# Routed attention and a gated FFN on one core: one-hot columns turned apart from the split keys and queries, values loaded from Pool's queue, a second FFN output bank

## The chip, the cores and the metric

The kernel runs on one core of a Trainium2 chip. The core has a matrix engine (PE, with its weight loads listed apart as PEld), three engines for elementwise work (DVE, ACT, POOL), a queue engine without arithmetic (SP), 16 DMA engines that all queues share, an on-chip memory of 128 partitions (SBUF), and an accumulator memory (PSUM) of eight banks of 128 partitions x 512 fp32, which PE alone writes with matmuls. Each engine runs its own instructions in order and waits for others by semaphores. The metric is the device time of one execution in microseconds.

## What is computed

Attention in which a query sees only the keys of its own cluster, followed by a gated feed-forward network. B = 4 batches, H = 8 heads, S = 768 positions, D = 64, 16 centroids for each head; 3072 tokens, model width 512, inner width 1536; all fp32.

```python
q_assign = np.argmax(np.einsum('bhsd,hcd->bhsc', q_n, c_n), axis=-1)
k_assign = np.argmax(np.einsum('bhsd,hcd->bhsc', k_n, c_n), axis=-1)
mask = q_assign[:, :, :, None] == k_assign[:, :, None, :]
scores = np.where(mask, scale * np.matmul(q, k.transpose(0, 1, 3, 2)), -1e9)
attn = np.exp(scores - scores.max(-1, keepdims=True))
x = tokens_of(np.matmul(attn / (attn.sum(-1, keepdims=True) + 1e-9), v))
gate = 1.0 / (1.0 + np.exp(-(x @ w_gate)))
return gate * (x @ w_val) @ w_out
```

The last line stands for `(gate * val) @ w_out`; `tokens_of` moves the heads side by side.

## The kernel before

**Clusters as extra rows.** For each head the kernel builds a tile T: 128 rows for each position, in chunks of 128 positions. Rows 0 to 63 are the key or query in fp16. Rows 64 to 127 first hold what fp16 lost of it (hi and lo, made by `split`: DVE casts, POOL subtracts). From all 128 rows PE computes the 16 logits of each position (`logits2`, L226, in the first batch, 36 matmuls for each pair of heads; `logits`, L240, later, 12 for each head). DVE picks the largest (`pick`, L252) and writes a one-hot of 16 columns for a key, and -1920 times its complement for a query, over the first 16 lo columns of the same position-major tile `hl`. Scores then use rows 0 to 79 of T, so the mask comes out of the same matmul. As `hl` is position-major and T is row-major, `turn` (L219) sends it through a DMA transpose from SP's queue. It does so twice for each tile: once for the logits, once more with the one-hots in it:

```python
SP.dma_start_transpose(out=T[key], in_=hl.rearrange("p c x -> p (c x)"))
```

**Steps.** `run_steps` goes over score steps. A step is one score matmul (128 keys x 384 queries, L399), an exponential on ACT (L404), and, two steps later, three matmuls with the values (L416). The first batch runs as 48 steps on the first halves of the queries (kind "A") and 48 on the second ("B"); each further batch has 96 steps, 12 for each head. In this count the second batch begins at step 96. After the last step of a head POOL normalises (L200), after each second head a DMA transpose from SP makes the FFN's input xA, xB or xT.

**What is hung between the steps.** `at(i, f)` puts work behind step i in program order: loads, splits, turns, logits, picks, sums of the values, weight loads. The order of each engine is the program order. In the first batch a pair of heads has one T of 18 chunks for A (12 of keys, 6 of queries) and one of 6 for B. From the second batch on, `head_prep` (L535) starts 30 steps ahead of use: split, four steps on the first turn, at 12 the logits, at 13 pick and second turn, both of 12 chunks. A pair's keys, queries and values are loaded 80 steps ahead from SP's queue. The weights come from POOL's queue (fp32 in memory, fp16 in SBUF): behind steps 8, 20, 25, 31 a third of gate and value weights each comes in four parts, behind 37 and 43 the output weights.

**FFN.** From step 60 on, matmuls of the FFN of finished tokens are spread between the steps (`ffn_run`, with a cost for each piece): gates (L281, tanh on ACT L287), values (L296, product on DVE L301), outputs in three parts of four matmuls (L313, eviction on ACT L322 or DVE L320, store from SP). What is left of the last batch runs after its attention.

**PSUM.** `ring` (L66) is a ring of five banks, used in turn by scores, gates, values, logits and value sums; a bank can be written again when its reader is done. `avp` has two banks for the products with the values, `op` (L68) one for the FFN output.

**Start.** PE warms up on 14 matmuls of zeros (`dummies`), the centroids are normalised (`centroid_prep`, L133), then come split, turns and logits of pairs 0 and 1.

## Time and profile before

| | |
|---|---|
| median of 2 runs | 420.66 us (419.72 and 421.6) |
| the profiled execution | 421.55 us, of which the span is 419.8 us |
| PE busy | 338.0 us, 81% of the span |
| ACT busy | 230.1 us, 55% |
| DVE busy | 172.8 us, 41% |
| POOL busy | 109.1 us, 26% |
| DMA, SP's queue | 51.17 MB, packets' time 57.2% of 16 engines' span |
| DMA, POOL's queue | 4.72 MB, 8.6% |

The span runs from the first instruction to the last; what lies around it is 1.75 us. Busy shares are means over stages that differ, so they are read by stage. A wait is idle time of an engine, put down to what ended it. A DMA share above 1 means that packets of several queues were under way on an engine at once. The granted clock of PE is given as a share of 2.4 GHz; 0.5 is 1.2 GHz.

### The profile page before, as it was taken

The page shows a single profiled execution, that of the slowest core. Times are in us where ns is not written, and L with a number is a line of the kernel's source. Part 1 is how long each engine was busy: PE and PEld are TensorE (multiplying, and loading weights), DVE is VectorE, ACT ScalarE, POOL GpSimd, SP SyncE. Part 2 cuts the span into 40 slices and gives each one's busy share as a digit, 9 for nine tenths or more (in the row PEclk, how much of TensorE's full clock was granted, in tenths as well). Part 3 has the DMA queues.
Part 4 walks back from the last instruction along what each step waited for, and adds up shares of the span by engine and source line. Part 5 has one row for each costly group of instructions (what it writes and reads, how often), then busy time and mean ns, then how long its engine had stood idle before and what let it go on. Part 6 is the DMA issues. An engine that isn't in the chain of part 4 may idle for free.

```text
span 419.8 us, 8423 instructions
## 1 busy us (share of the span) xinstructions
PE 338.0 (81%) x3129; PEld 205.4 (49%) x3129; DVE 172.8 (41%) x441; ACT 230.1 (55%) x524; POOL 109.1 (26%) x174
## 2 busy tenths in 40 slices
PE   5166801619999688768999989999999899899995
PEld 1135501406665355444456656664666566465552
DVE  1332301302573446463455646572656443133230
ACT  2034600527875667675577767775887678143230
POOL 1653520300433142351324242323233200000000
PEclk9565665556999989896999999999999999999999
DMA  8999999991677958797877688587465831200201
GB/s 298 267 164 131 171 182 164 123 243 39 161 163 172 202 108 196 144 183 146 175 168 193 153 161 229 107 207 138 96 123 96 147 84 20 69 27 0 78 0 75
DMA packets 135769, 58.78 MB, mean 140 GB/s; under 512 B 114736, under 2 KB 132656, under 8 KB 135728
## 3 DMA queue, kind: packets, MB, share of 16 engines
q1 hardware_dynamic: 128304, 51.17, 57.2%
q0 software_dynamic: 5792, 4.72, 8.6%
q10 hardware_dynamic: 1632, 2.36, 1.6%
q8 instruction: 24, 0.39, 0.4%
q14 instruction: 17, 0.14, 0.1%
HBM read 28.34 MB, written 6.29 MB: 83 GB/s over the span
## 4 chain that ended last, share of the span: by engine, by line
PE 49%; DMA 12%; DVE 2%; issue 1%; ACT 1%; SPq 0%; POOL 0%; DVEq 0%; ACTq 0%; POOLq 0%
PE o L313 13%; DMA T<-hl 12%; PE g L281 11%; PE v L296 11%; PE sc L399 8%; PE av L416 4%; PE lg L243 2%; ACT ob L322 1%; ACT es L404 1%; DVE ob L320 1%; DVE hl L265 0%; SPq L224 0%; DVE hT L301 0%; POOL hl L215 0%; PE vs_ps L167 0%
## 5 line engine op out<-in xcount | busy, mean ns | idle before, releaser
L404 ACT ACTIVATE es<-sc 128x384 f16<-128x384 f32 x384 | 174.6, 493 | 105.2 <-PE sc L399 88.0
L399 PE MATMUL sc<-T 80*128 80x384 f16 x384 | 128.4, 359 | 1.8 <-DMA T<-hl 1.8
L416 PEld LDWEIGHTS <-es 128*128 128x128 f16 x1152 | 86.5, 104 | 52.9 <-ACT es L404 7.9
L416 PE MATMUL av<-va,es 128*128 128x65 f16 x1152 | 104.9, 203 | 2.0 <-ACT es L404 1.3
L301 DVE SCALAR_TENSOR_TENSOR hT<-th,v 128x384 f16<-128x384 f32 x96 | 53.0, 553 | 91.2 <-PE av L416 49.5
L313 PE MATMUL o<-wo,hT 128*128 128x512 f16 x288 | 71.0, 378 | 5.5 <-DVE ob L320 2.9
L200 POOL TENSOR_TENSOR xp<-t,rec 128x384 f16<-128x384 f32 (+1 forms) x40 | 27.9, 697 | 160.8 <-DVE rec L197 136.3
L287 ACT ACTIVATE th<-g 128x384 f32<-128x384 f32 x96 | 47.3, 493 | 26.8 <-DVE hT L301 16.2
L281 PE MATMUL g<-xTb,wg 128*128 128x384 f16 x288 | 58.6, 325 | 0.1
L296 PE MATMUL v<-xTb,wv 128*128 128x384 f16 x288 | 58.6, 325 | 0.0
L281 PEld LDWEIGHTS <-wg 128*128 128x128 f16 x384 | 38.1, 99 | 22.6 <-issue 2.4
L296 PEld LDWEIGHTS <-wv 128*128 128x128 f16 x384 | 38.1, 99 | 22.2 <-issue 2.4
L215 POOL TENSOR_TENSOR hl<-kraw,hl 128x384 f16<-128x384 f32 x32 | 29.4, 924 | 73.9 <-issue 44.6
L313 PEld LDWEIGHTS <-hT 128*128 128x128 f16 x288 | 27.8, 97 | 33.2 <-issue 8.0
L399 PEld LDWEIGHTS <-T 80*128 80x128 f16 x384 | 39.2, 103 | 3.5 <-DMA T<-hl 2.7
L233 PE MATMUL lg<-cm,T 128*128 128x16 f16 x192 | 6.5, 175 | 42.1 <-DMA T<-hl 42.1
L215 POOL TENSOR_TENSOR hl<-qraw,hl 128x384 f16<-128x384 f32 (+1 forms) x40 | 30.4, 767 | 17.0 <-DVE hl L212 16.9
L195 DVE TENSOR_TENSOR t<-av,sv 128x390 f32<-128x390 f32 (+1 forms) x40 | 19.2, 480 | 25.3 <-PE av L416 25.3
L233 PEld LDWEIGHTS <-T 128*128 128x128 f16 x192 | 5.9, 105 | 43.3 <-DMA T<-hl 43.3
L243 PE MATMUL lg<-cm,T 128*128 128x32 f16 x288 | 11.1, 177 | 17.4 <-DMA T<-hl 17.2
L322 ACT ACTIVATE ob<-o 128x512 f32<-128x512 f32 x16 | 9.6, 597 | 26.2 <-PE o L313 26.1
L212 DVE CAST hl<-qraw 128x384 f16<-128x384 f32 (+1 forms) x40 | 13.9, 364 | 20.0 <-DMA T<-hl 20.0
(52 smaller groups left out, 206.5 us busy)
## 6 DMA issues: line engine op xcount, KB each, us to landing
kraw<-in_k_dram SPq DMA_DIRECT2D x16, 384.0 KB, 4.3
out_dram<-ob SPq DMA_DIRECT2D x24, 256.0 KB, 2.5
vraw<-in_v_dram SPq DMA_DIRECT2D x14, 384.0 KB, 5.2
qraw<-in_q_dram SPq DMA_DIRECT2D x12, 384.0 KB, 4.2
qraw<-in_q_dram ACTq DMA_DIRECT2D x4, 384.0 KB, 6.9
wg<-in_moe_w_gate_dram POOLq DMA_DIRECT2D x4, 384.0 KB, 9.6
wv<-in_moe_w_val_dram POOLq DMA_DIRECT2D x4, 384.0 KB, 11.9
wo<-in_moe_w_out_dram POOLq DMA_DIRECT2D x2, 768.0 KB, 12.7
```

What stands on the lines that cost most here:

```text
L195: DVE.tensor_tensor(t[:, 0:nq, :], av, sv, ALU.add)
L200: (eng or POOL).tensor_tensor(x, t[:, 0:nq, 0:64], bcast(rec[:, 0:nq], 64), ALU.mult)
L215: POOL.tensor_tensor(hl[:, o : o + m, 64:128], r, hl[:, o : o + m, 0:64], ALU.subtract)
L243: PE.matmul(out=lg[:, bass.ts(c, 32)], lhsT=T[key][:, c, :], rhs=cm[:, h].rearrange("p s n -> p (s n)"), start=True, stop=True,)
L281: PE.matmul(out=g[:, 0:n], lhsT=wg[fc // WQ][:, dc, fc % WQ, :], rhs=xT[:, dc, t0 : t0 + n], start=(dc == 0), stop=(dc == NDC - 1),)
L287: ACT.activation(th[:, 0:n], g[:, 0:n], AF.Tanh, scale=0.5)
L296: PE.matmul(out=w[:, 0:n], lhsT=wv[fc // WQ][:, dc, fc % WQ, :], rhs=xT[:, dc, t0 : t0 + n], start=(dc == 0), stop=(dc == NDC - 1),)
L301: DVE.scalar_tensor_tensor(hT[:, fc, 0:n], st[0][:, 0:n], 1.0, w[:, 0:n], ALU.add, ALU.mult)
L313: PE.matmul(out=o, lhsT=hT[:, fc, bass.ts(t, 128)], rhs=wo[fc // 6][:, fc % 6, :], start=(fc == 0), stop=(fc == NFC - 1),)
L399: PE.matmul(out=sc.rearrange("p (c t) -> p c t", t=128), lhsT=s["k"], rhs=s["q"], start=True, stop=True,)
L404: ACT.activation(es, sc, AF.Exp, scale=SCALE)
L416: PE.matmul(out=av[:, s["c0"] + i, :], lhsT=s["es"][:, bass.ts(i, 128)], rhs=VA[b, p][:, e, s["j"], :], start=(first and i == 0), stop=(la ...
```

## The change

**One-hots apart.** The one-hots no longer go into `hl`. `pick` writes them into tiles of their own, `oh` (three tiles of 128 x 6 chunks x 128, zeroed once), in which each head has 32 columns for keys and 32 for queries, two heads to a tile. Turned, they lie in rows 0 to 15, 32 to 47, 64 to 79 and 96 to 111 of `ohT`, and only those 16 rows are put into rows 64 to 79 of T, by `hop`: a DMA from SP of 16 partitions x 768 or 384 fp16 values. T is thus turned once for the logits and keeps rows 0 to 63.

- First pair: PE transposes 64 columns of `oh` at a time into PSUM, DVE and ACT copy 16 rows of it into T (`first_place`). No DMA.
- Pairs 1 to 3 of A, all of B: PE transposes, DVE copies PSUM to `ohT`, four or two hops (`a_place`, `b_place`).
- From the second batch on: one DMA transpose of 6 chunks for each pair of heads, then four hops (`pair_prep`). Splits begin 58 steps ahead of use (48 for the second head), keys and queries apart, the turn 9 steps after the split, the logits 20, the one-hots' turn 26 steps ahead of use, the hops 16 and 15.

**First batch.** T of A is now made for each head (9 chunks) instead of for each pair (18). The first head's lo part is subtracted on DVE. The order of the start is new: keys and queries of pair 0 are loaded first, those of pairs 2 and 3 behind the first turns, values from POOL's queue; 8 dummies, then 14 behind the centroids, and 2 twice. The weights are behind steps 14, 26, 30, 34, and 40 and 46. The splits of B are behind steps 20, 27, 34, 41, their turns 3 later, logits 14, hops 17. Later loads are 76 steps ahead of use.

**Pools.** `hl` 3 to 4, `T` 7 to 10 tiles (of 12 chunks at most, before 18), `ohT` two; the PSUM ring 5 to 4 banks, `op` 1 to 2.

SP's queue at the start of the program (k, q, v raw are the loaded inputs; T<-hl a turn; T<-ohT a hop). Before:

```order
L96 DMA cen<-in_centroids_dram 128x64
L93 DMA kraw<-in_k_dram 128x2x384 x3
L93 DMA vraw<-in_v_dram 128x2x384
L93 DMA kraw<-in_k_dram 128x2x384
L93 DMA vraw<-in_v_dram 128x2x384
L224 DMA_TRANSPOSE T<-hl 128x18x128 x7
L424 DMA_TRANSPOSE xA<-xp 128x3x128
```

After:

```order
L95 DMA kraw<-in_k_dram 128x2x384
L100 DMA cen<-in_centroids_dram 128x64
L95 DMA kraw<-in_k_dram 128x2x384
L222 DMA_TRANSPOSE T<-hl 128x9x128 x2
L95 DMA kraw<-in_k_dram 128x2x384
L95 DMA qraw<-in_q_dram 128x2x384
L222 DMA_TRANSPOSE T<-hl 128x9x128 x2
L95 DMA kraw<-in_k_dram 128x2x384
L95 DMA qraw<-in_q_dram 128x2x384
L287 DMA T<-ohT 16x768
L287 DMA T<-ohT 16x384
```

Two more hops and the four turns of heads 4 to 7 follow. The value loads are gone from here, four loads moved behind turns, and the turns of heads 4 to 7 stand behind the hops of pair 1.

POOL from the first values to the first weights (va are values cast to fp16, xp normalised outputs, hl lo parts). Before:

```order
L154 MEMSET va 128x12
L155 CAST va<-vraw 128x12x64
L215 TENSOR_TENSOR hl<-kraw,hl 128x6x64 x2
L215 TENSOR_TENSOR hl<-qraw,hl 128x3x64 x2
L200 TENSOR_TENSOR xp<-t,rec 128x3x64
L113 DMA wg_149<-in_moe_w_gate_dram 128x4x384
L113 DMA wv_150<-in_moe_w_val_dram 128x4x384
```

After:

```order
L95 DMA vraw<-in_v_dram 128x2x384 x2
L156 MEMSET va 128x12
L157 CAST va<-vraw 128x12x64
L202 TENSOR_TENSOR xp<-t,rec 128x3x64
L215 TENSOR_TENSOR hl<-kraw,hl 128x6x64
L215 TENSOR_TENSOR hl<-qraw,hl 128x3x64
L215 TENSOR_TENSOR hl<-kraw,hl 128x6x64
L215 TENSOR_TENSOR hl<-qraw,hl 128x3x64
L202 TENSOR_TENSOR xp<-t,rec 128x3x64
L114 DMA wg_137<-in_moe_w_gate_dram 128x4x384
L114 DMA wv_138<-in_moe_w_val_dram 128x4x384
```

The first weights now stand behind the output of the second head instead of the first, and the last two value loads stand ahead of them.

SP's queue in the second batch, one pair of heads. Before:

```order
L224 DMA_TRANSPOSE T<-hl 128x12x128 x2
L424 DMA_TRANSPOSE xTb<-xp 128x6x128
L224 DMA_TRANSPOSE T<-hl 128x12x128 x2
L93 DMA kraw<-in_k_dram 128x2x384
L93 DMA qraw<-in_q_dram 128x2x384
L93 DMA vraw<-in_v_dram 128x2x384
```

After:

```order
L95 DMA kraw<-in_k_dram 128x2x384
L95 DMA qraw<-in_q_dram 128x2x384
L95 DMA vraw<-in_v_dram 128x2x384
L645 DMA_TRANSPOSE ohT<-oh_153 128x6x128
L222 DMA_TRANSPOSE T<-hl 128x12x128
L444 DMA_TRANSPOSE xTb<-xp 128x6x128
L287 DMA T<-ohT 16x768 x4
L222 DMA_TRANSPOSE T<-hl 128x12x128
```

Four turns of 12 chunks became two, one of 6 chunks and four hops.

The diff, cut:

```diff
-    tp = pool("T", 7)
+    tp = pool("T", 10)
+    ohp = pool("oh", 2)
-    ring = pool("ring", 5, space=bass.MemoryType.PSUM)
+    ring = pool("ring", 4, space=bass.MemoryType.PSUM)
-    op = pool("op", 1, space=bass.MemoryType.PSUM)
+    op = pool("op", 2, space=bass.MemoryType.PSUM)
...
-        hl = HL[key]
-        for parts, alu in ((kparts, ALU.is_equal), (qparts, ALU.is_lt)):
-            for a, z in parts:
-                DVE.tensor_tensor(
-                    hl[:, a:z, 64:80], lg[:, a:z], bcast(mx[:, a:z], NCL), alu
-                )
-        for a, z in qparts:
-            DVE.tensor_scalar(hl[:, a:z, 64:80], hl[:, a:z, 64:80], MASK, None, ALU.mult)
+        for a, z, nh, key, o in parts:
+            DVE.tensor_tensor(
+                o,
+                lg[:, a:z].rearrange("p (h c) n -> p h c n", h=nh),
+                bcast(mx[:, a:z].rearrange("p (h c) -> p h c", h=nh), NCL),
+                ALU.is_equal if key else ALU.is_lt,
+            )
+            if not key:
+                DVE.tensor_scalar(o, o, MASK, None, ALU.mult)
...
+    def oh_turn_pe(oh, nc_):
+        ps = bank(NCH * 128, HP, name="oh_ps")
+        for c in range(nc_):
+            PE.transpose(ps[:, bass.ts(c, 128)], oh[:, c, :], identh)
+        return ps
+
+    def hop(src, slot, t, c0, n):
+        SP.dma_start(
+            out=t[64:80, c0 : c0 + n, :], in_=src[32 * slot : 32 * slot + 16, 0:n, :]
+        )
...
+    def first_place(e, oh):
+        ps = bank(NCH * 128, HP, name="oh_ps")
+        for c in range(NCH):
+            PE.transpose(ps[64 * e : 64 * e + 64, bass.ts(c, 128)], oh[:, c, 64 * e : 64 * e + 64], identh)
+        t = T["A", e]
+        pv = ps.rearrange("p (c t) -> p c t", t=128)
+        DVE.tensor_copy(t[64:80, 0:6, :], pv[64 * e : 64 * e + 16, :, :])
+        ACT.copy(t[64:80, 6:9, :], pv[64 * e + 32 : 64 * e + 48, 0:3, :])
...
+    def a_place(p):
+        ps = oh_turn_pe(st0["oh", p], NCH)
+        ot = ohp.tile([128, NCH, 128], HP, tag="ohT", name="ohT")
+        DVE.tensor_copy(ot.rearrange("p c t -> p (c t)"), ps)
+        for e in range(2):
+            hop(ot, 2 * e, T["A", 2 * p + e], 0, 6)
+            hop(ot, 2 * e + 1, T["A", 2 * p + e], 6, 3)
...
+    at(0, lambda: a_logits(1))
+    at(1, lambda: a_pick(1))
+    at(3, lambda: a_place(1))
+    at(4, lambda: (a_turn(4), a_turn(5)))
...
+    at(9, lambda: (a_turn(6), a_turn(7)))
+    at(12, lambda: a_logits(2))
...
+    at(14, lambda: load_w(0))
...
+    at(26, lambda: load_w(1))
     for p in range(NP):
-        s = 22 + 6 * p
+        s = 20 + 7 * p
         at(s, lambda p=p: b_split(p))
-        at(s + 2, lambda p=p: turn(("B", p), tbp, True))
-        at(s + 12, lambda p=p: b_logits(p))
-        at(s + 13, lambda p=p: b_pick(p))
-    at(25, lambda: load_w(2))
-    at(31, lambda: load_w(3))
-    at(37, lambda: load_wo(0))
-    at(43, lambda: load_wo(1))
...
+        at(s + 3, lambda p=p: b_turn(p))
+        at(s + 14, lambda p=p: b_logits(p))
+        at(s + 15, lambda p=p: b_pick(p))
+        at(s + 17, lambda p=p: b_place(p))
+    at(30, lambda: load_w(2))
+    at(34, lambda: load_w(3))
+    at(40, lambda: load_wo(0))
+    at(46, lambda: load_wo(1))
...
+        for e in range(2):
+            s = use - 58 + 10 * e
+            at(s, lambda e=e: sp(e, 0))
+            at(s + 4, lambda e=e: sp(e, 1))
+            at(s + 9, lambda e=e: turn((b, 2 * p + e), st["hl", e], tp))
+            at(s + 20, lambda e=e: lgt(e))
+            at(s + 21, lambda e=e: pk(e))
+        at(use - 26, ot)
+        at(use - 16, lambda: hops(0))
+        at(use - 15, lambda: hops(1))
```

## Rows read from the trace of the kernel before

**Rows 1.** Sums by stage: stretch; busy PE, PEld, DVE, ACT, POOL (count); PEclk, DMA, GB/s

```profile
0.00:26.90 26.90, 10.85 (x99) 5.14 (x99) 8.61 (x30) 2.97 (x4) 10.59 (x22) 0.68 0.96 249
26.90:99.80 72.90, 35.52 (x379) 24.34 (x380) 14.45 (x53) 28.53 (x61) 21.90 (x38) 0.56 1.02 163
99.80:127.90 28.10, 28.09 (x277) 17.82 (x276) 15.62 (x42) 21.40 (x50) 9.21 (x15) 0.98 0.56 138
127.90:203.00 75.10, 59.67 (x614) 36.68 (x610) 37.28 (x92) 49.28 (x118) 24.18 (x36) 0.89 0.78 168
203.00:357.40 154.40, 148.21 (x1461) 91.92 (x1462) 80.28 (x196) 111.68 (x260) 42.35 (x63) 1.00 0.66 137
357.40:419.80 62.40, 55.65 (x312) 29.51 (x308) 16.52 (x30) 16.23 (x32) 0.82 (x1) 0.99 0.12 42
```

**Rows 2.** The same sums for the score matmuls (L399) alone: PE, PEld

```profile
26.90:99.80 72.90, 27.19 (x61) 7.47 (x61) 0.56 1.02 163
```

**Rows 3.** Waits of PE, 26.9 to 99.8 us: total, times, longest

```profile
PE lg L233 <- DMA T<-hl: 32.0, 4, 18.7
```

**Rows 4.** Timeline: start, length, engine, line, instruction, count, idle before and releaser

```profile
18.70 1.13 PE L233 MATMUL lg<-cm,T 128*128 128x16 f16 x36 [9.21 <-DMA T<-hl]
...
22.41 2.72 PE L469 MATMUL wm<-warm 128*128 128x512 f16 x6
...
26.93 0.34 PE L399 MATMUL sc<-T 80*128 80x384 f16 x1 [1.79 <-DMA T<-hl]
...
35.17 0.94 POOL L113 DMA_DIRECT2D wg<-in_moe_w_gate_dram  x1
```

**Rows 5.** DMA from 13 to 34 us: rate in 40 slices; issues, us to landing

```profile
GB/s 377 375 372 190 181 205 222 215 214 179 209 218 217 217 171 1 0 5 201 209 150 1 9 168 290 286 289 290 288 93 102 215 214 216 220 158 0 0 103 216
...
T<-hl SPq DMA_TRANSPOSE x6, 4.7
```

**Rows 6.** DMA over the span: packets; POOL's queue; centroid load; landing of T

```profile
DMA packets 135769, 58.78 MB, mean 140 GB/s; under 512 B 114736, under 2 KB 132656, under 8 KB 135728
...
q0 software_dynamic: 5792, 4.72, 8.6%
...
cen<-in_centroids_dram SPq DMA_DIRECT2D x1, 32.0 KB, 2.1
...
DMA to landing us min/median/max: 2.7/4.1/20.6
```

**Rows 7.** DMA queues from 36 to 40 us: packets, MB, share

```profile
q0 software_dynamic: 476, 0.36, 92.0%
q1 hardware_dynamic: 17, 0.00, 0.4%
```

**Rows 8.** DMA queues from 60 to 68 us

```profile
q0 software_dynamic: 1513, 1.13, 89.7%
q1 hardware_dynamic: 1554, 0.40, 37.2%
```

**Rows 9.** Waits of PE, 128 to 203 us

```profile
PE lg L243 <- DMA T<-hl: 13.4, 6, 4.1
```

**Rows 10.** Waits of PE, 200 to 358 us, all

```profile
PE lg L243 <- DMA T<-hl: 3.8, 4, 1.6
PE o L313 <- DVE ob L320: 1.1, 2, 0.5
PE o L313 <- ACT ob L322: 1.0, 2, 0.5
PE av L416 <- ACT es L404: 0.3, 1, 0.3
```

**Rows 11.** Waits of PE, 358 to 420 us

```profile
PE o L313 <- DVE ob L320: 1.6, 2, 0.8
PE o L313 <- ACT ob L322: 1.4, 2, 0.7
```

**Rows 12.** Groups by line: busy, mean ns, idle before; the longest form on DVE

```profile
L161 DVE TENSOR_REDUCE vs<-vraw 128x128 f16<-128x768 f32 x12 | 17.6, 1468 | 0.0
```

More of the change, by code (lines that the diff above doesn't have):

```diff
@@ L95 @@
     cen = const.tile([128, D], FP, name="cen")
+    load(SP, "k", 0, 0)
+    load(ACT, "q", 0, 0)
     SP.dma_start(out=cen, in_=centroids.rearrange("h c d -> (h c) d"))
[L97 to L101 removed]
+    load(SP, "k", 0, 1)
+    load(ACT, "q", 0, 1)
     WQ = 3
@@ L475, in a_logits @@
     def a_logits(p):
-        logits2(("A", p), [(2 * p, [*range(0, 6)]), (2 * p + 1, [*range(6, 12)]),
-                           (2 * p, [12, 13, 14]), (2 * p + 1, [15, 16, 17])])
+        st0["lg", p] = logits2(sum((a_groups(2 * p + e, s) for s in range(2) for e in range(2)), []))
     def a_pick(p):
-        pick(("A", p), [(0, 12)], [(12, 18)])
-        turn(("A", p), tp, False)
+        oh = st0["oh", p] = new_oh()
+        pick(st0["lg", p], [(0, 12, 2, True, oh_view(oh, 0, 2, 2, 6)),
+                            (12, 18, 2, False, oh_view(oh, 1, 2, 2, 3))])
@@ L522, with b_place @@
-    at(20, lambda: v_sum_pe(0, 3))
-    at(20, lambda: load_w(1))
+        oh = st0["boh", p] = new_oh()
+        pick(st0["blg", p], [(0, 6, 2, False, oh_view(oh, 0, 2, 1, 3))])
+    def b_place(p):
+        ps = oh_turn_pe(st0["boh", p], 3)
+        ot = ohp.tile([128, 3, 128], HP, tag="ohT", name="ohT")
+        DVE.tensor_copy(ot.rearrange("p c t -> p (c t)"), ps[:, 0:384])
+        for e in range(2):
+            hop(ot, e, T["B", p], 3 * e, 3)
+    dummies(8)
+    centroid_a()
+    a_split(0, DVE)
@@ new lines @@
+    a_turn(0)
+    a_split(1, POOL)
+    a_turn(1)
+    DVE.tensor_copy(identh, ident)
+    centroid_b()
+    for i in range(3):
+        POOL.memset(ohs[i], 0.0)
+    load(POOL, "v", 0, 0)
+    load(SP, "k", 0, 2)
+    load(SP, "q", 0, 2)
+    a_split(2, POOL)
+    load(POOL, "v", 0, 1)
+    a_split(3, POOL)
+    a_turn(2)
+    a_turn(3)
+    load(SP, "k", 0, 3)
+    load(SP, "q", 0, 3)
+    dummies(14)
+    oh0 = new_oh()
+    first_logits(0, oh0)
+    dummies(2)
+    first_logits(1, oh0)
+    dummies(2)
@@ new lines, with pair_prep, sp, lgt @@
+        at(s + 14, lambda p=p: b_logits(p))
[5 more added lines that the diff above has]
+    at(46, lambda: load_wo(1))
+    def pair_prep(b, p, use):
+        st = {}
+        def sp(e, side):
+            if side == 0:
+                st["hl", e] = hlp.tile([128, 12, 128], HP, tag="hl", name="hl")
+            hl, r = st["hl", e][:, 6 * side : 6 * side + 6], RAW["kq"[side], b, p][:, e]
+            DVE.tensor_copy(hl[:, :, 0:64], r)
+            POOL.tensor_tensor(hl[:, :, 64:128], r, hl[:, :, 0:64], ALU.subtract)
+        def lgt(e):
+            st["lg", e] = logits(T[b, 2 * p + e], 2 * p + e, 12)
+        def pk(e):
+            if e == 0:
+                st["oh"] = new_oh()
+            pick(st["lg", e], [(0, 6, 1, True, oh_view(st["oh"], 2 * e, 1, 1, 6)),
+                               (6, 12, 1, False, oh_view(st["oh"], 2 * e + 1, 1, 1, 6))])
+        def ot():
+            st["ot"] = ohp.tile([128, NCH, 128], HP, tag="ohT", name="ohT")
+            SP.dma_start_transpose(out=st["ot"], in_=st["oh"].rearrange("p c x -> p (c x)"))
+        def hops(e):
+            for s in range(2):
+                hop(st["ot"], 2 * e + s, T[b, 2 * p + e], 6 * s, 6)
+        for e in range(2):
+            s = use - 58 + 10 * e
[7 more added lines that the diff above has]
+        at(use - 15, lambda: hops(1))
+        at(use - 20, lambda: v_cast(b, p))
+        at(use - 10, lambda: st.update(f=v_sum(b, p)))
+        at(use - 6, lambda: st["f"]())
```

168 lines of the change are left out of this document (77 added, 91 removed).

## The prediction

> **What bounds it now.** I read the sums by stage first, because the kernel has four different limits. Score steps are counted from 0: one step is one score matmul with its exponential and its products with the values. In [rows 1] six stages are cut at the start of a step. Before step 0 (26.9 us) PE is busy for 10.85 us. Steps 0 to 60 [rows 2] take 72.9 us with PE busy for 35.52, the clock at 0.56 and the DMA share at 1.02: this stage waits for transfers. Steps 61 to 95 (28.1 us, PE 28.09) are PE's. The second batch, steps 96 to 191 (75.1 us, PE 59.67, clock 0.89), has holes again. Batches three and four (154.4 us, PE 148.21) and the rest (62.4 us, 55.65) are nearly full of PE.
>
> Next the waits of PE in each stage. In steps 0 to 60 it waits 32.0 us in four waits for a turned T, 18.7 us at once [rows 3]; in the second batch 13.4 us in six such waits [rows 9]; in the third and fourth 3.8 us, and 2.1 us for the output bank's eviction [rows 10]; at the end 3.0 us for that bank [rows 11].
>
> Why T comes late, the DMA rows show. A turn lands in 4.7 us for 18 chunks while only turns run [rows 5], 2.7 at the least and 20.6 at the most over the kernel [rows 6]. Between 36 and 40 us the queue of the weight loads moved 476 packets and the one that carries the turns 17, although a turn had been issued [rows 7]; between 60 and 68 us they moved 1513 and 1554, of 1.13 and 0.40 MB [rows 8]. So the turns are starved while weights load, and those load from 35.17 us [rows 4] on. The totals are in the page: 4.72 MB on the weights' queue, and 114736 packets under 512 B [rows 6], which is 133 for each of the 864 chunks of 128x128 that are turned.
>
> **Start, and steps 0 to 60.** Now the first logits run at 18.70 us, after 9.21 us of waiting for the first turn; pick and second turn follow, and step 0 starts at 26.93 [rows 4]. After: keys and queries of pair 0 go first on two queues and are cast before the centroids are finished, so the first turn (9 chunks, between 2.7 and 4.7 us, I take 3.4) is issued at about 7 and lands at 10.5. PE then stands behind 14 dummies that follow the centroid transpose at about 9: at the 0.45 us of the six in [rows 4], 6.3 us, until 15.3. Logits 0.6, picks, six PE transposes for each head, copies of 16x768 (no such row; between nothing and the 1.47 us of the longest DVE form [rows 12]; I take 0.9, it is a copy) and the next dummies add 5: step 0 at about 20, bounds 16 and 24. Step 1 stands behind the logits of pair 1, whose turns are issued behind the zeroing of three tiles and two value loads on POOL: about 21.
>
> That 7 us is not all kept, since the stage ends with the transfers. Weights start at step 14 instead of 8. Steps 1 to 12 take 0.5 us each, place(1) must pass PE, DVE and SP before the turns of heads 4 and 5 are issued (SP is in order), and step 12 holds PE for those: I get step 14 at 32 us, so the weights start 3 us earlier than 35.17. From there the bill before was: weights 4.72 MB at 1.13 MB in 8 us = 33.4 us; six loads of the second batch, 2.36 MB at the start's 249 GB/s = 9.5; 78 chunks (18 of the last A turn, 48 B, 12 x) at 215 GB/s, the level of [rows 5], 0.15 each = 12. That is 55 of the 64.6 us from 35.2 to 99.8, so 10 us were gaps. After: 33.4, 9.5, 48 chunks (24 B, 12 x, 12 of the second batch's first head, whose turn now comes at step 47) = 7.3, and 16 hops of 12 or 24 KB, 0.3 MB, 1 us by bytes; each should land like the 32 KB of centroids in 2.1 us [rows 6], and all are issued nine steps or more ahead of their use. That is 51. Of the gaps I take off 2, for round trips that need no second turn. Sum: 3 + 4 + 2 = 9 us earlier at step 61. Bounds: 0 (the turns of B still wait for the end of the weights, and the hops behind them in SP's order) and 24 (steps 0 to 60 at 0.67 each from 20 us on).
>
> **Steps 61 to 95.** PE is full there; nothing is removed from it, 0.
>
> **Second batch.** Before, a head's first turn stands 8 steps ahead of its logits; after, 11, and the second turn of 12 chunks becomes, for two heads together, one of 6 chunks ten steps ahead of the hops, and these 16 ahead of use. Turned chunks per batch fall from 192 to 120. 13.4 us of waits: with 11 steps of 0.6 us = 6.6 us against a landing of 4.1 [rows 6] plus 1 to 2 behind outputs in SP's queue I leave 2.4, so 11 go. The clock of 0.89 comes back towards 1.00: 11% of 59.67 us of PE is 6.6, part of which lies in the waits; I take 3. Against it the ring has four banks. Batches three and four use 312 banks (192 scores, 96 gates and values, 24 others) in 154.4 us, 0.49 us each, so losing one takes 0.49 us from the time a reader has, and a reader that is late costs at most that. Readers are late where DVE has a long piece of work, the 1.47 us sum of values [rows 12] or a pick: three for each pair, 2 us for four pairs as the value between nothing and 12 x 0.49 = 6. Sum 12 us, bounds 5 and 17.
>
> **Batches three and four.** The waits for T (3.8) and for the output bank (2.1) go; eight pairs pay up to 24 x 0.49 = 12 us for the ring, I take 5. Sum 1 us, bounds 6 gained and 6 lost.
>
> **The rest.** Four waits for the output bank, 3.0 us [rows 11], go; only gates and values use the ring, each read within its 0.65 us. 3 us. What follows the last matmul stays.
>
> Values on POOL's queue, the PE transposes of the B part and the centroid edits lie inside the stages above. Without their cover the four value loads would cost POOL the 0.9 us of a weight issue [rows 4] each.
>
> **A rule against the rows.** The starving in [rows 7] and the even counts in [rows 8] do not say the same. The Trainium skill (DMA: Bandwidth & Descriptors, Queues, rings and completion order) states that each DMA engine goes round the queues it has work for, a packet at a time. [rows 8] agrees (1554 to 1513), [rows 7] does not (17 to 476); by that rule the fair case below would be the likely one.
>
> **Sum.** 9 + 0 + 12 + 1 + 3 = 25 us off the profiled execution's 421.55 (span 419.8 and 1.75 around it): 396.5. The median of the two runs is 420.66, 0.2% lower; on its scale 396.
>
> **Rivals.**
> - *Fair turns*: the queues share as in [rows 8], 194 small packets per us. From about 41 us the hardware queue has 48 chunks of 128 packets and six loads of 256, 7680 packets, 40 us: step 61 near 82 instead of 91. 387 us. For it [rows 8], against it [rows 7].
> - *Weights alone rule the first batch*: turns and hops of B wait for the last weight, step 61 comes only 2 us earlier: 403. For it the 32.0 us of [rows 3].
> - *The second batch still waits*: SP's queue, held by outputs and x turns, issues turns as late as now; 3 us gained there: 405. For it that a hop now waits in SP's order for DVE and for a turn; against it the ten steps.
> - *Four banks are too few* (slower): if each of the some 500 banks from step 61 to the last score comes late by 0.08 us, 40 us are lost, which takes the gain (32 us without the ring's own 7) and 2% more; from there it decides. 439 us at 0.1 us. Against it: with five banks no wait of PE in [rows 10] is for a score's, gate's or value's bank, and readers of 0.5 us fit in four banks of 0.49.
>
> **Chances.** The forecast 0.42, fair turns 0.22, weights alone 0.12, second batch still waits 0.12, four banks 0.05, others 0.07, several small losses together that leave it within 2%. About 2% is what a measurement of this kernel can tell from no change, here 412.2 and 429.1 us. Faster 0.88, the same 0.07, slower 0.05. The range 381 to 410 takes in the first four cases, with 5 to 6 us beyond the outer ones; the forecast's own range is 390 to 402.
>
> **What would show it.** Right: step 0 near 20 us, weights issued near 32, step 61 near 91, the waits of PE for T in the second batch under 3 us and its clock near 1.00, no wait for the output bank at the end, waits of PE for ACT's or DVE's readers of 0.1 to 0.5 us new in batches three and four. Wrong: step 34 or 41 (the logits of B, behind turns under the weights) holding PE until all weights have landed; the logits of heads 2 to 5 holding PE at the start for longer than 9 us; a T of the second batch landing over 7 us after its issue; hops landing in more than 5 us and holding a score.

## The result and the profile after

The changed kernel takes 379.84 us (median; 379.63 and 380.05), the kernel before 420.66: a ratio of 0.903 (95% interval 0.894 to 0.912), 40.8 us less. The direction was forecast, the size was not: 25 us, and a range that ended at 381.

The profiled execution has a span of 378.3 us. The sums by stage, cut at the same steps as [rows 1] (step 0, 61, 96, 192, last score); stretch, then busy PE, PEld, DVE, ACT, POOL (count), PEclk, DMA share, GB/s:

```profile
0.00:21.00 21.00, 12.98 (x81) 5.65 (x82) 10.19 (x28) 3.71 (x6) 10.03 (x21) 1.00 0.81 220
21.00:82.10 61.10, 39.19 (x458) 27.26 (x458) 23.35 (x79) 29.44 (x63) 29.72 (x47) 0.61 1.04 192
82.10:111.60 29.50, 29.50 (x291) 18.52 (x289) 16.88 (x47) 21.58 (x51) 9.29 (x15) 0.94 0.58 136
111.60:170.90 59.30, 53.00 (x613) 33.44 (x610) 35.51 (x93) 48.21 (x118) 24.45 (x36) 1.00 0.77 178
170.90:319.50 148.60, 147.34 (x1437) 91.11 (x1438) 74.30 (x180) 111.28 (x259) 39.32 (x59) 1.00 0.48 111
319.50:378.30 58.80, 54.98 (x312) 29.49 (x308) 16.48 (x30) 16.21 (x32) 0.83 (x1) 1.00 0.13 45
```

Against [rows 1], in us:

| stage | before | after | gain | forecast |
|---|---|---|---|---|
| up to step 61 | 99.9 | 82.1 | 17.8 | 9 |
| (of it: up to step 0) | 26.9 | 21.1 | 5.8 | 7, "not all kept" |
| steps 61 to 95 | 28.1 | 29.5 | -1.4 | 0 |
| second batch | 75.1 | 59.3 | 15.8 | 12 |
| batches 3 and 4 | 154.2 | 148.4 | 5.8 | 1 |
| the rest | 62.5 | 58.9 | 3.6 | 3 |

PE's waits after (total, times, longest), first in steps 0 to 60, where [rows 3] had 32.0, 4, 18.7:

```profile
PE lg L229 <- DMA T<-hl: 10.9, 6, 4.6
PE sc L419 <- DMA T<-ohT: 4.5, 3, 3.3
PE lg L238 <- DMA T<-hl: 3.5, 1, 3.5
PE oh_ps L283 <- DVE oh L265: 2.1, 2, 1.3
```

Then in the second batch, where [rows 9] had 13.4, 6, 4.1:

```profile
PE vs_ps L169 <- DVE vs L163: 2.2, 4, 0.7
PE lg L238 <- DMA T<-hl: 2.1, 4, 0.7
```

In the stage after the last score no wait is left; the four of [rows 11] are gone.

How large a difference can be read from one stage: six kernels, the changed one among them, have its first batch in the same program order (two of them with other banks), and their step 61 comes between 81.2 and 84.7 us. For the second batch a second execution of the kernel before took 73.4 in place of 75.1 us. Its batches 3 and 4 took 154.2 and 154.9 us, but 156.3 to 158.8 in three kernels below that have the same code there (e4, e10, e12); with the changed kernel's code and banks there they lie between 148.3 and 149.0. So up to 3 us in the first stage and under 2 in the second batch are scatter, and in batches 3 and 4 of the kernel before some 5.

### The profile page after: what moved, and what is told of

Same layout as the page of the kernel before. It is cut to its first block, busy times and chain, and to the rows that moved or that the text cites. A ratio compares the mean times of both kernels' runs of the same rounds, so it can differ in the third digit from the quotient of the medians.

```text
span 378.3 us, 8520 instructions
## 1 busy us (share of the span) xinstructions
PE 337.0 (89%) x3177; PEld 205.5 (54%) x3177; DVE 176.7 (47%) x455; ACT 230.4 (61%) x527; POOL 113.6 (30%) x179
## 4 chain that ended last, share of the span: by engine, by line
PE 68%; DMA 14%; DVE 7%; issue 4%; POOL 3%; ACT 1%; SPq 1%; POOLq 0%; DVEq 0%
PE o L333 16%; PE v L316 15%; PE g L301 15%; DMA T<-hl 12%; PE sc L419 11%; PE av L436 6%; PE lg L238 2%; DMA T<-ohT 2%; PE wm L489 2%; DMA cen<-in_centroids_dram 1%; DVE hT L321 1%; POOL hl L215 1%; DVE vs L163 1%; DVE hl L212 1%; DVE t L197 1%
## 5 line engine op out<-in xcount | busy, mean ns | idle before, releaser
L419 PE MATMUL sc<-T 80*128 80x384 f16 x384 | 124.3, 348 | 5.8 <-DMA T<-ohT 4.5
L436 PEld LDWEIGHTS <-es 128*128 128x128 f16 x1152 | 84.6, 102 | 51.0 <-ACT es L424 6.1
L436 PE MATMUL av<-va,es 128*128 128x65 f16 x1152 | 102.3, 200 | 1.4 <-ACT es L424 0.7
L419 PEld LDWEIGHTS <-T 80*128 80x128 f16 x384 | 38.3, 100 | 5.4 <-DMA T<-ohT 4.2
L632 POOL TENSOR_TENSOR hl<-kraw,hl 128x384 f16<-128x384 f32 x24 | 22.0, 917 | 31.4 <-issue 24.8
L632 POOL TENSOR_TENSOR hl<-qraw,hl 128x384 f16<-128x384 f32 x24 | 21.9, 913 | 20.7 <-DVE hl L631 20.5
L163 DVE TENSOR_REDUCE vs<-vraw 128x128 f16<-128x768 f32 x12 | 17.6, 1466 | 0.0
L340 DVE TENSOR_SCALAR ob<-o 128x512 f32<-128x512 f32 x8 | 5.5, 692 | 25.6 <-PE o L333 25.6
L252 DVE TENSOR_TENSOR lgs<-lg,lglo 128x192 f32<-128x192 f32 x24 | 8.5, 355 | 17.8 <-ACT lglo L244 17.3
```

Source lines behind the costliest of these rows:

```text
L163: DVE.tensor_reduce(s[:, :, 0:64], RAW["v", b, p].rearrange("p h c d -> p h d c"), AX.X, ALU.add)
L419: PE.matmul(out=sc.rearrange("p (c t) -> p c t", t=128), lhsT=s["k"], rhs=s["q"], start=True, stop=True,)
L436: PE.matmul(out=av[:, s["c0"] + i, :], lhsT=s["es"][:, bass.ts(i, 128)], rhs=VA[b, p][:, e, s["j"], :], start=(first and i == 0), stop=(la ...
L632: POOL.tensor_tensor(hl[:, :, 64:128], r, hl[:, :, 0:64], ALU.subtract)
```

## The experiments: the first batch

Each kernel is given with its median, the ratio to the kernel before on the same chip, and the stages of its profiled execution. A line number in rows is that of the kernel shown.

**e0_before**, the kernel before again, to see whether its stall repeats.

> The kernel before, profiled once more. Theory A (the starving I read was an accident of one execution: packets of both queues held for 2 to 4 us near 36 and 56 us): the first turn of B, which took 20.6 us to land, lands in 8 to 12 us this time and the packet counts of the two queues between 36 and 40 us are no longer 476 to 17. Theory B (the order of issue holds it: the turn stands behind three loads on its own queue and beside six weight loads on the other): it lands in 18 to 23 us again and step 35 starts at 70 to 74 us, whatever the packets did. Time 419 to 422 either way.

420.52 us; step 61 at 99.9 as the first time, the stall at step 34 again, and the turn that had taken 20.6 us to land took 20.8 (theory B; that turn is the second one of the last A pair, not the first one of B). But the packets from 36 to 40 us are not those of [rows 7] (476 to 17):

```profile
q0 software_dynamic: 447, 0.34, 80.7%
q1 hardware_dynamic: 289, 0.07, 8.9%
...
T<-hl SPq DMA_TRANSPOSE x1, 10.3
```

The starving was an episode of one execution; the turn issued there took 10.3 us all the same (10.5 the first time), of which SP's queue held it for 6.7 (7.0).

**e7_first_batch_dma**: the changed kernel with the first batch's one-hots (pairs 1 to 3 of A, all of B) turned by DMA, followed by the same hops.

```diff
-        ps = oh_turn_pe(st0["oh", p], NCH)
         ot = ohp.tile([128, NCH, 128], HP, tag="ohT", name="ohT")
-        DVE.tensor_copy(ot.rearrange("p c t -> p (c t)"), ps)
+        SP.dma_start_transpose(out=ot, in_=st0["oh", p].rearrange("p c x -> p (c x)"))
...
```

> The changed kernel with the one-hots of pairs 1 to 3 and of B in the first batch turned by DMA (6 or 3 chunks from SP's queue) instead of by PE and a DVE copy; the first pair as it is. Theory A (a turn beside weight loads takes 9 to 11 us to land, and the hops wait for it): step 61 6 to 12 us later, 386 to 392. Theory B (only bytes count, 30 chunks of 0.15 us): 2 to 4 us later, 382 to 384.

401.69 us (0.9534, 0.948 to 0.9587), step 61 at 102.9: 20.8 us later, far beyond both theories. PE's waits from step 0 to 60:

```profile
PE sc L419 <- DMA T<-ohT: 29.3, 4, 13.5
PE lg L229 <- DMA T<-hl: 5.1, 4, 2.8
```

A turn and a hop, one behind the other and both beside the weights, are what scores then wait for. That is more than the kernel before had (one DMA leg), so 20.8 overstates what the change gained.

**e10_before_pe_turn** asks from the other side: the kernel before with this one part; in the steps `place` stands two behind each pick.

```diff
         pick(("A", p), [(0, 12)], [(12, 18)])
-        turn(("A", p), tp, False)
...
-        turn(("B", p), tbp, False)
+
+    def place(key, n):
+        for a in range(0, n, 6):
+            ps = bank(768, HP, name="oh_ps")
+            for c in range(6):
+                PE.transpose(ps[0:16, bass.ts(c, 128)], HL[key][:, a + c, 64:80], identh)
+            DVE.tensor_copy(
+                T[key][64:80, a : a + 6, :], ps[0:16].rearrange("p (c t) -> p c t", t=128)
+            )
...
```

> The kernel before with one edit: the first batch's one-hot columns are turned by PE (six transposes into a bank, one DVE copy into T per six chunks) in place of the second DMA turn, two steps behind their pick; weights, loads, ring of five and one output bank stay. Theory (the second turn's wait carries the first stage): step 61 comes at 80 to 86 us in place of 99.9, the total is 401 to 407 us. Rival (the first turns beside the weights hold as long, and the earlier loads or the later weights are needed too): step 61 at 92 or later, the total 413 or more. In between: both have a part.

415.33 us (0.9849, 0.9804 to 0.9894); step 61 at 90.6, between the two, but the total is the rival's: of the 9.3 us gained up to step 61, batches 3 and 4, which the edit does not touch, take back 4.6 (158.8). Its step 0 came at 28.1, so steps 0 to 60 took 62.5 us against 72.9 before and 61.1 after:

```profile
28.10:90.60 62.50, 39.24 (x442) 25.63 (x442) 20.48 (x65) 27.05 (x61) 22.55 (x39) 0.65 0.93 152
```

PE's waits for T there, against the 32.0 of [rows 3]:

```profile
PE lg L234 <- DMA T<-hl: 19.5, 4, 8.9
```

So this part alone takes 10.4 us off steps 0 to 60, of the 11.8 that the change takes off them. Before, SP's queue shows why a removed turn is worth that much:

```profile
50.33 11.62 SPq L224 DMA_TRANSPOSE T<-hl  x1
```

This is the second turn of the last A pair (18 chunks). It holds SP's queue for 11.62 us, although the last event of another engine that the profile finds for it came within its first 2.6 us, and lands at 70.92; the first turn of the first B tile is the next entry of that queue, goes out at 61.99 and lands at 71.71. On that one step 34 waits 18.7 us [rows 3], and POOL's two loads of output weights, behind it in program order, go out late. Start and length on POOL, before and after:

```profile
74.92 0.89 POOL L119 DMA_DIRECT2D wo<-in_moe_w_out_dram  x1
...
78.64 0.88 POOL L119 DMA_DIRECT2D wo<-in_moe_w_out_dram  x1
```

```profile
56.91 0.89 POOL L120 DMA_DIRECT2D wo<-in_moe_w_out_dram  x1
...
61.81 0.88 POOL L120 DMA_DIRECT2D wo<-in_moe_w_out_dram  x1
```

After, the last weights land at 75.6 instead of 93.0, though the first start no earlier (35.91, before 35.17).

**e4_before_weights_late, e5_after_weights_early, e12_before_pe_turn_late** move the weight loads: the kernel before with the changed kernel's steps, the changed kernel with the steps of before, and e10 with the later steps.

```diff
-    at(8, lambda: load_w(0))
+    at(14, lambda: load_w(0))
...
-    at(43, lambda: load_wo(1))
+    at(46, lambda: load_wo(1))
```

> The kernel before with nothing changed but the steps behind which the weights are loaded: 14, 26, 30, 34, 40, 46 as after the change, instead of 8, 20, 25, 31, 37, 43. Theory A (what ended the first batch's stall is that the first turn of B, behind step 24, now goes ahead of the second weights): step 34 is no longer held for 19 us, step 61 comes 8 to 12 us earlier, 409 to 413. Theory B (the halved turned chunks did it): weights that start later only end later, 420 to 425.

417.29 us (0.9934, 0.9887 to 0.998): step 61 at 94.1, 5.8 earlier, the total 3.6 less, between the two theories.

> The changed kernel with the weights behind the steps of before: 8, 20, 25, 31, 37, 43. Theory A (the first turns of B must go ahead of the weights): steps 34 and 41 are held again, 386 to 390. Theory B (the queues share, the weights' bytes are the bill of this stage): weights that start some 3 us earlier end earlier, 376 to 380.

383.62 us (0.9098, 0.9039 to 0.9156), between the two; step 61 at 85.4, just past the scatter. As its step 0 came at 19.5, steps 0 to 60 took 4.8 us longer than in the changed kernel:

```profile
19.50:85.40 65.90, 40.99 (x459) 28.46 (x459) 23.17 (x79) 29.52 (x63) 29.76 (x47) 0.59 1.16 183
```

> The kernel before with two edits: the first batch's one-hots turned by PE (as in e10) and the weight loads behind the changed kernel's steps 14, 26, 30, 34, 40, 46. Start, rings and later batches stay as before. Theory (steps 0 to 60 are shortened by these two alone, and the rest of the 17.8 us comes from the earlier start): steps 0 to 60 take 59 to 61 us as in the changed kernel (61.1), step 61 at 87 to 89, the total 410 to 413. Rival (PE's turning takes all that there is to take, later weights add nothing to it): steps 0 to 60 take 62 to 63 us, step 61 at 90 to 91, the total 414 to 416.

415.59 us (0.9842, 0.9805 to 0.988): steps 0 to 60 take 63.7 us, not less than e10's 62.5. The rival held: in the kernel before later weights help while second turns are there (e4) and add nothing once PE turns (e12). That does not carry over to the changed kernel, where the early weights cost something (e5); why they do there and not in e10 was not tested.

**e6_no_weight_loads** leaves out the weight loads of the changed kernel (the weights are set to zero on DVE), so that the FFN's output is zero.

> The changed kernel without the weight loads: DVE writes zeros over the weight tiles in their places, so the FFN's output is zero; all other work is done. Theory A (steps 0 to 60 are bound by transfers and the weights are most of them): step 61 at 62 to 66 us instead of 82, total 360 to 364. Theory B (steps 0 to 60 are bound by the chain of turn, logits, pick, place and hop on PE, DVE and SP): step 61 at 76 to 82, total 374 to 380.

367.58 us (0.8718, 0.8654 to 0.8782): step 61 at 71.4, steps 0 to 60 about 9 us shorter. Between the two again. Weights cost at least that much (DVE writes the zeros in the same stage, 31.2 us busy for 23.4); the rest of the stage is not theirs:

```profile
19.50:71.40 51.90, 38.73 (x459) 26.57 (x459) 31.21 (x89) 28.79 (x63) 22.05 (x37) 0.68 0.66 143
```

Even here the clock is 0.68 and PE is busy for 38.73 of 51.90 us.

**e13_late_start** puts 28 for 14 dummies ahead of the first logits; **e9_start** 4, and clears two of the three one-hot tiles later.

> The changed kernel with 28 in place of 14 warming matmuls ahead of the first logits: step 0 near 27 us, where the kernel before has it (26.9), instead of 21.1. Theory (the earlier start is carried whole to step 61): step 61 at 86.5 to 88.5 us, the total 384 to 387. Rival (the transfers of the first batch fix step 61, and the start is hidden behind them): step 61 at 82 to 84, the total 379.5 to 382. Half way: only some of it is carried.

383.29 us (0.9067, 0.9017 to 0.9118). Step 0 came at 24.0, 2.9 later (less than I meant), step 61 at 86.7, 4.6 later and past the scatter, the total 3.5 more, a little under the theory's range. A later start is not hidden behind the transfers; how much of an earlier one is kept, this does not settle to better than the scatter.

> The changed kernel with 4 in place of 14 warming matmuls ahead of the first logits, and two of the three one-hot tiles cleared by Pool behind the splits of heads 2 and 3 in place of ahead of them. Theory (the start is held by the 14 matmuls and by the slowed DVE step ahead of the centroids' transpose, and all that follows is tied to the steps): first logits near 14 in place of 17.4 us, step 0 near 18, the total 376.5 to 378.5 us. Rival (the weights and the turns of heads 2 to 7 fix when the first batch is done): step 0 earlier, but step 61 at 81.5 to 82.5 as now, the total 379 to 381; or the clock is granted low for more of the first stage and the total is higher.

378.32 us (0.8977, 0.8935 to 0.9019). The first logits ran 5.5 us earlier (11.98 for 17.45), step 0 only 1.6 (19.4), step 61 0.9 (81.2). What stood in between, on PE:

```profile
11.98 0.67 PE L229 MATMUL lg<-cm,T 128*128 128x16 f16 x18
...
17.46 1.40 PE L513 MATMUL oh_ps<-identh,oh 128*64 128x128 f16 x12 [2.60 <-DVE mx L256]
...
19.42 0.53 PE L419 MATMUL sc<-T 80*128 80x384 f16 x1
```

DVE's picks became the late ones. Two of their instructions took 3.73 and 2.73 us:

```profile
13.59 3.73 DVE L265 TENSOR_SCALAR oh<-oh 128x48 f16<-128x48 f16 x1
14.58 2.73 DVE L256 TENSOR_REDUCE mx<-lg 128x9 f32<-128x144 f32 x1
```

In the changed kernel the same two take 0.17 and 0.29. Both end at 17.3 us, where a run of POOL's instructions ends (two subtracts, the two moved clears, a small clear and a cast; 13.69 to 17.28). And the clock was granted at 0.50 (1.2 GHz) from the first logits to past step 0, where the changed kernel has 1.00, so the first score takes 0.53 us instead of 0.32: of the rival, the part on the clock came true. It is the fastest kernel here that does all the work, but not told apart from the changed one.

**e8_values_sp**: the changed kernel with the four value loads on SP's queue, `load(SP, "v", 0, 0)` and so on.

> The changed kernel with the first batch's four value loads back on SP's queue at the same places of the program. Theory (the queue of these loads is worth nothing by itself): 379 to 382 us, step 0 at 21 to 22 us, step 61 at 81 to 83. Rival (on SP's queue they hold the turns of heads 2 to 7 behind them): step 61 at 85 or later, the total 383 or more.

380.62 us (0.9022, 0.8975 to 0.907), step 0 at 21.2, step 61 at 84.0: nothing that can be told from the changed kernel.

## The experiments: batches two to four, and the banks

**e3_lead8** gives the changed kernel the short lead: the first turn 8 steps ahead of the logits, as before, instead of 11.

```diff
-            at(s + 9, lambda e=e: turn((b, 2 * p + e), st["hl", e], tp))
+            at(s + 12, lambda e=e: turn((b, 2 * p + e), st["hl", e], tp))
```

> The changed kernel with the first turn of each head of batches two to four issued 8 steps ahead of its logits, as before the change, instead of 11. Theory A (the lead removed the 13.4 us of waits in the second batch): most of it returns, 8 to 12 us slower, 388 to 392. Theory B (the lighter queue did it: fewer and shorter turns on SP): at most 2 us slower, 380 to 382.

398.76 us (0.9483, 0.9434 to 0.9532), beyond theory A's range: the second batch 68.0 us (8.7 more), batches 3 and 4 156.6 (8.2 more). PE waits for T again, 8.7 us in four waits in the second batch, and the clock falls:

```profile
112.60:180.60 68.00, 56.70 (x614) 35.27 (x611) 34.98 (x93) 48.75 (x118) 24.41 (x36) 0.92 0.67 156
```

It looked as if the lead were the cause. Five more kernels tested it.

**e11_two_turns** gives the changed kernel two whole second turns of 12 chunks for each pair, in place of the joint turn and the hops; **e14_lead8_two_turns** does both edits.

```diff
-            SP.dma_start_transpose(out=st["ot"], in_=st["oh"].rearrange("p c x -> p (c x)"))
+            for e in range(2):
+                SP.dma_start_transpose(
+                    out=T[b, 2 * p + e], in_=st["hl", e].rearrange("p c x -> p (c x)")
+                )
...
```

> The changed kernel, but in batches 2 to 4 the one-hot columns go back into hl, and two whole second turns (12 chunks each) per pair of heads go out at the step where the one joint turn stood; no hops. First batch, leads and rings stay. Theory (the lead alone removed the waits of batches 2 to 4): at most 2 us more than the changed kernel, 380 to 383 us, batch 2's steps 59 to 61 us. Rival (fewer chunks turned matters by itself, the queue is too full with 48 chunks per pair): batch 2's steps 63 us or more, the total 387 or more.

385.45 us (0.9133, 0.9078 to 0.9187), between the two; the second batch 59.8 us, which is the theory's, batches 3 and 4 151.3 (2.9 more).

> The changed kernel with both: the first turn of a head 8 steps ahead of its logits (as in e3) and two whole second turns of 12 chunks for each pair in place of the joint turn and the hops (as in e11). The first batch, rings and loads stay. Theory (with the short lead the second turns, which stand ahead of first turns in the queues, cost what the second batch gained beyond the lead): the second batch takes 73 to 76 us as in the kernel before (75.1), the total 403 to 409. Rival (the second turns are harmless at either lead): 68 to 69.5 us as with the short lead alone (68.0), the total 398 to 402; then the rest of the 15.8 us has another cause.

401.18 us (0.9528, 0.9488 to 0.9568), the second batch 69.2 us: the rival. The number of turned chunks, 120 or 192 in a batch, is worth about 1 us there at either lead, and some 3 in batches 3 and 4 (148.4 to 151.3; 156.6 to 159.7).

**e15_before_lead11** gives the kernel before the long lead, `s = use - 33` for `use - 30`, with logits and pick at their old steps.

> The kernel before with the split and first turn of each head of batches 2 to 4 three steps earlier, so that the turn stands 11 steps ahead of its logits; logits, pick and second turn stay at their steps. Theory (the lead alone): the second batch takes 66 to 68 us in place of 75.1, batches 3 and 4 some 5 us less, the total 404 to 409. Rival (three hl tiles are too few for it, a split then waits for the second turn that frees its tile, and the wait only moves): second batch 72 us or more, the total 414 or more.

411.57 us (0.9752, 0.9716 to 0.9788), between the two: the second batch 70.9 us, only 4.2 less than before, batches 3 and 4 150.9, 3.3 less. PE still waits 11.4 us for T. What SP's queue waits for in the second batch, in the kernel before and then in e15:

```profile
SPq L224 <- DVE hl L269: 28.6, 8, 4.5
```

```profile
SPq L224 <- DVE hl L269: 23.0, 8, 4.6
```

L269 ends the pick. A head's second turn stands in SP's queue and waits for its pick, eight times in eight heads; the next head's first turn is the entry behind it, also with the long lead, where the two fall on one step. So turn, logits, pick and second turn of one head must pass before the next head's first turn goes out: a loop. It went round in 9.4 us for each head (75.1 / 8); the changed kernel needs 7.4 (59.3 / 8). The changed kernel still has such a wait, for the joint turn (L645) and so once for two heads, of 18.8 us in all:

```profile
SPq L645 <- DVE rec L199: 9.0, 2, 4.6
SPq L645 <- DVE oh L265: 6.0, 2, 3.5
SPq L645 <- DVE hl L631: 3.8, 1, 3.8
```

**e16_before_second_later** cuts that loop alone: the second turn four steps later, so that it stands behind the next head's first turn. **e17_before_both** does so with the long lead.

```diff
             pick((b, h), [(0, 6)], [(6, 12)])
-            turn((b, h), tp, False)
 
         at(s + 13, pk)
+        at(s + 17, lambda: turn((b, h), tp, False))
```

> The kernel before with the second turn of each head in batches 2 to 4 four steps later, 13 steps ahead of use, so that it stands behind the next head's first turn in SP's queue and not ahead of it; lead, logits and pick stay. Theory (in the kernel before each head's first turn stands behind the previous head's second turn, which waits for that head's pick: a loop of 9.2 us per head): with the loop cut the second batch takes 66 to 69 us in place of 75.1, the total 407 to 412. Rival (the short lead of 8 steps holds the logits anyway): second batch 73 us or more, the total 418 or more.

399.98 us (0.9482, 0.9432 to 0.9531), better than the theory's best. The second batch takes 59.5 us, as in the changed kernel, batches 3 and 4 149.3, with two turns of 12 chunks for each head, five ring banks, one output bank and the lead of 8:

```profile
127.90:187.40 59.50, 52.33 (x613) 33.53 (x610) 37.39 (x92) 47.59 (x118) 24.20 (x36) 1.00 1.00 203
```

Waits of PE and of SP's queue there, the first row of each:

```profile
PE lg L243 <- DMA T<-hl: 5.1, 6, 2.3
```

```profile
SPq L224 <- POOL hl L215: 9.1, 5, 2.6
```

SP's longest waits are now for POOL's splits; the one for L269 is no longer among those listed, PE's wait fell from 13.4 to 5.1, and the clock is 1.00.

> The kernel before with both: the split and first turn three steps earlier (as in e15) and the second turn four steps later (as in e16). Theory (the lead and the loop through SP's queue are the whole of the second batch's gain): the second batch takes 59 to 62 us as in the changed kernel (59.3), batches 3 and 4 150 to 152 us, the total 400 to 405. Rival (three hl tiles, 12-chunk turns or something else in the changed kernel are needed): second batch 65 us or more, the total 408 or more.

395.47 us (0.9375, 0.9335 to 0.9414): the second batch 55.7 us, 3.6 less than the changed kernel's, PE's wait for T 1.5 us; batches 3 and 4 149.0:

```profile
125.90:181.60 55.70, 52.08 (x614) 33.47 (x611) 35.96 (x93) 47.42 (x118) 24.15 (x36) 1.00 1.04 219
```

The total is better than the theory's range, and 26.2 us less than the kernel before on the same chip: a split and two turns moved by a few steps there, with the one-hots still in `hl`, bring well over half of what the whole change brings.

**e1_ring5_op1, e2_ring4_op1**: the changed kernel with the old banks (ring five, output one), and with both small.

> The changed kernel with the PSUM pools as before: ring of five banks, one output bank. My prediction (the ring's fifth bank is worth 7 us, the second output bank 5): about 378. Rival (four banks cost nothing, the second output bank gives its 5 us, waits of 2.1 and 3.0 us come back): about 385.

384.21 us (0.9138, 0.9093 to 0.9183), near the rival's; second batch 59.2, batches 3 and 4 149.0, the rest 62.5.

> The changed kernel with a ring of four banks and one output bank, so seven PSUM banks. Against the run with five and one it prices the ring's bank alone: my prediction 7 us slower than that run; rival: the same within 1 us. Against the changed kernel it prices the second output bank: 5 us slower by both.

387.71 us (0.9213, 0.9179 to 0.9247), 3.5 more than e1 and 7.9 more than the changed kernel; 59.8, 151.2 and 62.5. So the fifth ring bank is worth 0.6 + 2.2 = 2.8 us from the second batch on, and the second output bank, by e2 against the changed kernel, 0.5 + 2.8 + 3.6 = 6.9. The waits of PE at the end return with one bank as they were in [rows 11]:

```profile
PE o L333 <- DVE ob L340: 1.6, 2, 0.8
PE o L333 <- ACT ob L342: 1.4, 2, 0.7
```

## Why the prediction fell short, step by step

**What bounds the kernel** was read rightly: PE waits for turned tiles in two stages, and these waits fell, from 32.0 to 18.9 us (hops included) in the first and from 13.4 to 2.1 in the second. Why the tiles were late was not. For the first stage I took shares of packets and bytes as the cause, for the second the lead. The views named another: in the rows of SP's own waits, which I did not use, second turns wait for their picks 28.6 us in one batch, each ahead of the turn that the next logits need.

**The start** was right in its size: step 0 at 21.05 (about 20), the first turn issued at 7.42 and landed 3.5 us later (7, and 3.4). In part that is luck. The centroids' transpose, and with it the 14 dummies, came later than the 9 and 15.3 us of the sum, and what follows the dummies took 3.6 us where the sum had 5:

```profile
11.42 0.45 PE L145 MATMUL ct_ps<-ident,c 128*128 128x128 f32 x1 [6.00 <-DVE c L143]
...
17.45 0.60 PE L229 MATMUL lg<-cm,T 128*128 128x16 f16 x18
```

"That 7 us is not all kept" finds no support: in e13 a later start is carried to step 61, so I count the 5.8 us gained there whole.

**Steps 0 to 60.** The failed step is the bill of transfers, "78 chunks ... 0.15 each" against 48: it priced the removed second turns at their bytes, 30 chunks, 4.5 us. They were worth 10.4 (e10), since they held up SP's queue and with it the first turn of B and the last weights. (The bill also counts time twice: the weights' 1.13 MB in 8 us [rows 8] were measured with 0.40 MB of turns moving beside them, and the turns are then added. Both sides of the difference have that term.) The weights "3 us earlier" did not come (35.9, not 32), and would not have brought time: e5 lost some with earlier weights, and e10, with the weights of before, was no slower than e12. Hops were priced at 2.1 us to landing, and those beside the weights took 5.7 (48 to 64 us):

```profile
T<-ohT SPq DMA_DIRECT2D x6, 12.0 KB, 5.7
```

Scores waited 4.5 us for them, and the first turn of the second batch took 12.3 us to land: two of the signs of being wrong came true here, and the stage was still 8.8 us better than forecast. If parts from different kernels may be added, the 17.8 us are 5.8 of the start, 10.4 of PE's turning, and 1.6 that no run isolates and that lies within the scatter.

**Fair turns**, the rival, named step 61 near 82, and it came at 82.1. Its number held, in part by chance: it had no term for the turns that held SP's queue. Its mechanism is only half supported. Beside the weights, packets from 48 to 64 us after:

```profile
q0 software_dynamic: 3243, 2.44, 105.9%
q1 hardware_dynamic: 2340, 0.62, 25.7%
...
T<-hl SPq DMA_TRANSPOSE x3, 10.1
```

1.4 to 1, with SP's queue not always full. The Trainium skill (DMA: Bandwidth & Descriptors, Queues, rings and completion order) has each DMA engine go round its queues by packets; this row comes near it, as [rows 8] did, and the 476 to 17 of [rows 7] did not repeat; that a packet of these rows (752 and 265 bytes in the mean) is one of that page's is not shown by any run. But the sharing was as even in the kernel before, so it is no gain of the change.

**The second batch.** "11 of 13.4 waits" and the clock's return to 1.00 came true (2.1 us are left), and the size, 12 against 15.8, was not far off. The reason I gave, the lead of 11 steps, is only about half of it. What the lead is worth hangs on the order in SP's queue: 4.2 us in the old order (e15), 3.8 once the order is mended (e17 against e16), 8.7 in the changed kernel (e3). There a joint turn still waits for a pick ahead of the next pair's first turn, once for two heads, and the lead covers that wait. The order by itself gives 15.6 in the kernel before (e16), with no longer lead. What the changed kernel gains beyond its lead (75.1 to 69.2, e14) I put down to one such wait for two heads in place of one for each; that was not tried by itself. The clock was priced at 3; PE's busy time fell by 6.7 (59.67 to 53.00).

**Batches 3 and 4.** I counted 3.8 us of visible waits and 5 for the ring. Cutting the loop gives 4.9 there (e16), the output bank 2.8 (2.1 in my sum), and the fifth bank costs 2.2: 5.5 together, against 5.8 measured, though the scatter of the kernel before is as large, so that the agreement proves little. The lead, priced here only by the 3.8 us of waits, is worth 8.2 in the changed kernel (e3). The ring was the mis-sized term; I had charged a wait for each late reader, and readers were hardly late: waits for them did come, as forecast, but few (0.9 us in four after), and the longest for a gate, value or score is 0.3 us.

**The rest**: 3 forecast, 3.6 measured; e1 and e2 show it to be the output bank. **Steps 61 to 95**: forecast 0, measured -1.4; the clock was 0.94 there and PE full. The five other kernels with the same first batch took 28.1 to 29.1, so this is not settled and small.

**The rivals that failed.** "Weights alone" (403): step 61 came 17.8 us earlier and not 2, and without any weights steps 0 to 60 are some 9 us shorter (e6), so the stage is not theirs alone. "The second batch still waits" (405, 3 us gained there) would have come near with the lead alone in the old order (e15, 4.2). "Four banks too few": the bank costs 2.8 us in all.

**The range** ended too high because its terms were not independent: one thing, second turns that stand less in the way of first ones in SP's queue, gained in three stages at once, while I let one case at a time be the good one.

## What to carry over

A DMA that waits for a computed result, put into an in-order queue ahead of one that does not, can tie the two into a loop (here 15.6 us of a stage of 75.1); look at the queue's own waits before counting bytes or adding lead. Price a removed transfer by what stands behind it in its queue, not by its size. And where one edit serves several stages, let their gains rise and fall together in the range. On from here, the changed kernel with its joint turn moved behind the next pair's first turn was not tried; e17's 55.7 us for the second batch lets me estimate that it has some 3 us left there.

## What the runs showed of the chip that I had not expected

- A turn can hold SP's queue long after the last event of another engine that the profile finds for it: the 18-chunk turn beside the weights for 11.62 us, where one at the start, with no weights under way, took 2.78. The changed kernel has such a turn too, the first of the second batch, of 12 chunks, behind three loads; such a turn mostly takes 1.4 to 1.5 us there. What holds them no view names.

```profile
67.16 9.21 SPq L222 DMA_TRANSPOSE T<-hl  x1
```

- Turns beside the weights take about 10 us to land whatever the packet counts say: 10.5 us in the kernel before with 476 to 17 packets, 10.3 in e0_before with 447 to 289 (some 7 of each in SP's queue), 10.1 us (median of three) after with 3243 to 2340; without weights 3.3 in e6 (median of five, 40 to 64 us).
- The two scalings of the centroids on DVE (L143) took 2.24 us in the changed kernel, with POOL's three clears of 768 columns beside them. DVE's row, and POOL's:

```profile
9.03 2.24 DVE L143 TENSOR_SCALAR c<-cen,r 128x64 f32<-128x64 f32 x2
```

```profile
9.10 2.10 POOL L565 MEMSET oh<- 128x768 f16 x3
```

In e9_start, with one clear there, they took 0.89 us, in the kernel before, with none, 0.42, and each time DVE ends with the last clear (11.27 and 11.20, 9.89 and 9.81). In e9_start DVE's step of 0.17 us then took 3.73 us, up to the end of a run of six instructions of POOL. That DVE's steps wait for POOL's is what these suggest; it wasn't tried by itself.
